# Both inputs of a two-part kernel transposed by DMA instead of by TensorE

## The chip, the core and the metric

The kernel runs on one core of a Trainium2 chip. The core has five engines that work side by side, each in the order of its own instruction queue: TensorE (PE; PEld are its weight loads), VectorE (DVE), ScalarE (ACT), GpSimd (POOL) and SyncE (SP), which here only issues DMAs. Matmul results land in PSUM, from where VectorE or ScalarE copies them to SBUF. The metric is the device time of one execution in microseconds (us).

## What is computed

Two independent parts share the launch, and their outputs are put side by side. Each has its own x of 2048 tokens by 448 features in bf16.

```python
# part A: a diagonal state space model, 448 complex states
Lam_bar = exp(dt * Lam);  B_bar = ((Lam_bar - 1) / Lam)[:, None] * Bmat
Bu = einsum("bld,pd->blp", x, B_bar)
h_t = Lam_bar * h_{t-1} + Bu_t                      # over 2048 tokens
y = 2 * einsum("blp,dp->bld", h, Cmat).real + x * Dskip
# part B: attention with 16 heads of 28, each token over 8 keys, 2 apart
q, k, v = split(x @ wqkv)
logits = q . k[s - 2 w] * scale, w = 0..7;  attn = softmax(logits)
out_b = (sum_w attn * v[s - 2 w]) @ wo
out = concat([y, out_b], -1)
```

## The kernel before, in words

TensorE contracts over the partitions (at most 128), so every product with x needs x with its features on the partitions. The kernel loads x with the tokens on the partitions (`load_x` of each part, L95 and L303; tiles `xb_sb` and `xa_sb`, which share the buffer "xin" one after the other) and turns it with TensorE: `transp` (L153 and L476) transposes eight blocks of 128 tokens by 112 features into a PSUM tile `pt_x` and one copy (`ev`, L73) takes it to `xT`. The 448 features stand as KT = 4 slabs of KP = 112.

**Part B** works in four chunks of 512 tokens. `proj_t` (L161, matmul L165) makes eight tiles of q and k per chunk, each 112 features by 512 tokens from four matmuls over the slabs; the weights `wn` come in three loads, k first (`load_w`). `qk` (L184) multiplies q with eight shifted views of k on VectorE (`pr`, L192), sums over each head's 28 features by matmuls with a matrix of ones (`lg`, L196), transposes the logits for their maximum (`pt_m`, L209; L210), subtracts it and takes exp. `proj_v` (L172) makes v for every sixteenth token per j; `halo` (L180) copies rows between partitions by DMA. `norm` (L220) normalises; `pv` (L236) multiplies and sums over the eight keys on VectorE (L249, L252), and `tail` (L256) transposes the result (`pt_o`), copies it (`oT`) and multiplies by wo (`wo_ps`, L269).

**Part A** puts token 16p + j on partition p. The 448 complex states are seven groups m of 64 states, real and imaginary parts on 128 partitions. `setup_b` (L445) multiplies B by a scale (`matg`) into `Bcat`, the weights of `local`. `local(b)` (L488, matmul L496) makes for each m a PSUM tile of 4 x 128 tokens (j = 4a + b) from four matmuls over the slabs, to which b = 1 and b = 3 add carried states (L499, L502); ScalarE copies it to `h[b]`. `setup_c` (L456) transposes C. `scan` (L511) runs the recurrence over 128 partition blocks on VectorE, `groups` (L556) and `correct(b)` (L571) bring its result back into the states, and `y` (L599) sums x times Dskip (a diagonal matrix `Dg`, L604) and the states times C (L607).

**What sets the order.** The body (L615) writes the order of the program; a scheduler keeps it as a priority and lets a later instruction go ahead on an engine when an earlier one is not ready, and then each engine's queue is fixed. `weave` (L662) runs a generator `main` and puts k steps of a `fill` between its steps: the projections and transposes of the next chunk go between the steps of `qk`, v between those of `qk(3)`, the transposes of part A's x between those of `local`. All large loads are issued on SyncE's queue in program order: B's x and weights, B and C of part A (`load_bc`), wo, later A's x. The small parameters go on ScalarE's queue (`load_params`). PSUM tiles come in three sets of buffers: "mm" (3), "pt" (2) and "lg" (3).

Of the kernel before, what the change touches and what calls it, by code (L numbers as in the profile page):

```python
# [31 lines left out]
PL = 64  # L32
MA = 4
# [54 lines left out]
class PartB:  # L88
# [6 lines left out]
    def load_x(self, n0, n1):  # L95
        if n0 == 0:
            self.x_sb = self.pool.tile([NCH, T, D], bf16, name="xb_sb", tag="xin")
        xv = self.B_x[0].rearrange("(n p) d -> p n d", p=NCH)
        self.nc.sync.dma_start(self.x_sb[:, n0:n1, :], xv[:, n0:n1, :])

    def load_w(self, which):
        if which == 1:
            self.wn = self.pool.tile([KP, KT, 3, D], bf16, name="wqkv_nat", tag="wn")
        v = self.B_wqkv.rearrange("(k p) (w c) -> p k w c", p=KP, w=3)
        self.nc.sync.dma_start(self.wn[:, :, which, :], v[:, :, which, :])
# [46 lines left out]

    def transp(self, n, eng):  # L153
        nc, cx = self.nc, self.cx
        pt = cx.ps([KP, KT, 2, NCH], bf16, "pt_x", "pt")
        for i in range(2):
            for k in range(KT):
                nc.tensor.transpose(pt[:, k, i, :], self.x_sb[:, n + i, k * KP:(k + 1) * KP], cx.ident[:])
        cx.ev(eng, self.xT[:, :, n * NCH:(n + 2) * NCH], pt[:].rearrange("p k i c -> p k (i c)"))
# [115 lines left out]
class PartA:  # L275
# [7 lines left out]
    def load_params(self):  # L283
        nc, pool = self.nc, self.pool
        self.prow = pool.tile([3 * NM, 2, PL], bf16, name="prow")
        self.drow = pool.tile([KT, KP], bf16, name="drow")
# [3 lines left out]
        nc.scalar.dma_start(self.drow[:], self.A_Dskip.rearrange("(k p) -> k p", p=KP))  # L290

    def load_bc(self):
        nc, pool = self.nc, self.pool
        self.bX = pool.tile([NCH, NM, D], bf16, name="bX")
        nc.sync.dma_start(self.bX[0:PL], self.A_Bre.rearrange("(m p) d -> p m d", p=PL))
        nc.sync.dma_start(self.bX[PL:NCH], self.A_Bim.rearrange("(m p) d -> p m d", p=PL))
        self.cn = pool.tile([KP, KT, NM, 2, PL], bf16, name="cn", tag="cn")
        for ri, src in enumerate((self.A_Cre, self.A_Cim)):
            v = src.rearrange("(a p) (m q) -> p a m q", p=KP, q=PL)
            for a in range(KT):  # L300
                nc.sync.dma_start(self.cn[:, a, :, ri, :], v[:, a])
# [16 lines left out]
    def params(self):  # L318
# [13 lines left out]
        ptd = self.cx.ps([KP, KT], bf16, "pt_d", "lg")  # L332
        nc.tensor.transpose(ptd[:], self.drow[:], ident[0:KT, 0:KT])
        dsk = sm("dsk", (KP, KT))
# [63 lines left out]
    def params_g(self):  # L398
        nc, G, ident = self.nc, self.nc.vector, self.cx.ident
        lre, lim, rden, Scat, dsk = self.lre, self.lim, self.rden, self.Scat, self.dsk  # L400
        la_re, la_im = self.pw_re[:, 0, :], self.pw_im[:, 0, :]

        def sm(name):
            return self.pool.tile([NCH, NM], f32, name=name)

        lm1, g_re, g_im, t1 = (sm(n) for n in ("lm1", "g_re", "g_im", "t1"))
        G.tensor_scalar(lm1[:], la_re, -1.0, None, op0=ALU.add)
        G.tensor_tensor(g_re[:], lm1[:], lre, op=ALU.mult)
        G.tensor_tensor(t1[:], la_im, lim, op=ALU.mult)
# [35 lines left out]
    def setup_b(self, engs):  # L445
        nc, cx, pool = self.nc, self.cx, self.pool
        self.Bcat = pool.tile([KP, KT, NM, NCH], bf16, name="Bcat")
        for i in range(NM):
            pt = cx.ps([KP, KT, NCH], f32, "pt_b", "pt")
            for k in range(KT):  # L450
                nc.tensor.matmul(pt[:, k, :], lhsT=self.bX[:, i, k * KP:(k + 1) * KP], rhs=self.mats["g"][:, i, :],
                                 start=(k == 0), stop=(k == KT - 1), skip_group_check=True)
            cx.ev(engs[i % len(engs)], self.Bcat[:, :, i, :], pt[:])
            yield
# [14 lines left out]
    def alloc(self):  # L469
        pool = self.pool  # L470
        xa = pool.tile([KP, 4, KT, 4, NCH], bf16, name="xaT", tag="xT")
        self.xT = {i: xa[:, i] for i in range(4)}
        u01 = pool.tile([NCH, 2, NM, 4 * NCH], bf16, name="u01", tag="q")
        self.h = [u01[:, 0], u01[:, 1], None, None]

    def transp(self, b, eng):  # L476
        nc, cx = self.nc, self.cx
        t_ = self.xT[b]
        for a in range(0, 4, 2):
            pt = cx.ps([KP, KT, 2, NCH], bf16, "pt_x", "pt")  # L480
            for i in range(2):
                for k in range(KT):
                    nc.tensor.transpose(pt[:, k, i, :], self.x_sb[:, 4 * (a + i) + b, k * KP:(k + 1) * KP],
                                        cx.ident[:])
            cx.ev(eng, t_[:, :, a:a + 2, :], pt[:])
            yield

    def local(self, b):  # L488
        nc, cx = self.nc, self.cx
        if b == 2:  # L490
            u23 = self.pool.tile([NCH, 2, NM, 4 * NCH], bf16, name="u23", tag="xin")
            self.h[2], self.h[3] = u23[:, 0], u23[:, 1]
        for m in range(NM):
            ps = cx.ps([NCH, 4 * NCH], f32, "u_ps", "mm")
            for k in range(KT):
                nc.tensor.matmul(ps[:], lhsT=self.Bcat[:, k, m, :], rhs=self.xT[b][:, k].rearrange("p a c -> p (a c)"),  # L496
                                 start=(k == 0), stop=(b % 2 == 0 and k == KT - 1))
# [13 lines left out]
    def scan(self):  # L511
# [6 lines left out]
        pc = [pool.tile(tab, bf16, name=f"pc{i}") for i in range(2)]  # L518
        psn = [pool.tile(tab, bf16, name=f"psn{i}") for i in range(2)]
# [79 lines left out]
    def y(self, a, b):  # L599
# [3 lines left out]
        for k in range(KT):  # L603
            nc.tensor.matmul(ps[:, k * KP:(k + 1) * KP], lhsT=self.xT[b][:, k, a, :], rhs=self.Dg[:, k, :],  # L604
# [10 lines left out]
def body(ctx: ExitStack, tc: tile.TileContext, A_x, A_Lre, A_Lim, A_Bre, A_Bim, A_Cre, A_Cim, A_logdt, A_Dskip,  # L615
# [25 lines left out]

    def transp(c):
        for n in range(0, 4, 2):
            b.transp(4 * c + n, "AV"[(n // 2) % 2] if c == 0 else "A")
            yield
# [48 lines left out]
    for b_ in (1, 0, 2):  # L694
        for _ in a.correct(b_, "A"):
# [39 lines left out]
```

## Time and profile before

| | |
|---|---|
| runs, median of 2 | 178.68 us (177.88 to 179.47) |
| the profiled execution | 177.29 us, its span 175.3 us |
| granted TensorE clock | 1.00 |
| busy: TensorE, VectorE, ScalarE, GpSimd | 159.6, 132.6, 108.9, 5.6 us |
| read from HBM, written | 6.89 MB, 3.67 MB |

The span runs from the first to the last instruction of the profiled execution. A row of the time line gives the start, the duration, the engine, the line of the kernel, the operation, the tiles written and read with partitions x elements, the count, and in brackets how long the engine had been idle before and what released it. In a row of the stretches stand the length, then the busy time (and the instructions) of PE, PEld, DVE, ACT and POOL, the granted clock, the mean busy share of the DMA engines and what they moved in GB/s. Matmuls are pipelined and their ends are modelled, so what a group of them costs is better read from the start of the next.

### The profile page before, as it was taken

Reading aid. Unit: us, or ns where it says so; the run is one execution under the profiler, and the core shown is the slowest. Engines: PE = TensorE matmul, PEld = TensorE weight load, DVE = VectorE, ACT = ScalarE, POOL = GpSimd, SP = SyncE. Lnnn points to the kernel's source line nnn. Section 1 sums busy time; section 2 is a strip of 40 time slices with the busy share of each in tenths; the row PEclk is TensorE's granted clock in tenths of the full one; section 3 lists DMA queues with packets and bytes.
Section 4 is the critical chain, followed back from the end, with each engine's and each line's share of the span. In section 5 each row is a group of like instructions: output and inputs, shape, how many; then the busy total and the mean of one; then the engine's idle time right before and its main releaser. Section 6 shows DMA issues by size and latency. Waiting matters only on the chain.

```text
span 175.3 us, 2965 instructions
## 1 busy us (share of the span) xinstructions
PE 159.6 (91%) x1171; PEld 90.8 (52%) x1175; DVE 132.6 (76%) x189; ACT 108.9 (62%) x183; POOL 5.6 (3%) x37
## 2 busy tenths in 40 slices
PE   7589798799799999999999999969999999999981
PEld 4355333445444766676565444746755455554550
DVE  1299998999996894039999999999999999900000
ACT  2279444775744876788899654356238739738382
POOL 8400000000000000000000000000000000000000
PEclk9999999999999999999999999999999999999999
DMA  5999851000370004170000000002111230140113
GB/s 155 291 297 179 90 119 30 0 4 0 87 332 0 6 0 109 50 200 8 0 4 0 0 0 0 4 0 77 33 52 52 79 108 26 52 132 30 52 54 105
DMA packets 16589, 12.36 MB, mean 70 GB/s; under 512 B 7219, under 2 KB 16065, under 8 KB 16575
## 3 DMA queue, kind: packets, MB, share of 16 engines
q1 hardware_dynamic: 16504, 12.16, 26.2%
q8 instruction: 9, 0.15, 0.4%
q14 instruction: 5, 0.04, 0.1%
q10 hardware_dynamic: 71, 0.01, 0.0%
HBM read 6.89 MB, written 3.67 MB: 60 GB/s over the span
## 4 chain that ended last, share of the span: by engine, by line
PE 51%; DVE 32%; ACT 10%; DMA 3%; issue 1%; ACTq 1%
PE y_ps L607 11%; PE qk_ps L165 11%; DVE pvb L252 9%; DVE pvt L249 8%; PE v_ps L177 7%; PE wo_ps L269 5%; PE lg L196 5%; DVE pr L192 4%; DMA drow<-in_A_Dskip_dram 3%; PE co L577 2%; ACT u L588 2%; DVE pvb L249 2%; PE y_ps L604 2%; ACT oT L264 2%; PE gt L566 1%
## 5 line engine op out<-in xcount | busy, mean ns | idle before, releaser
L192 DVE TENSOR_TENSOR pr<-qT,kT 112x2048 bf16<-112x2048 bf16 x32 | 37.0, 1219 | 0.5 <-ACT qT L77 0.5
L165 PE MATMUL qk_ps<-xbT,wqkv_nat 112*112 112x512 bf16 x128 | 32.3, 386 | 1.4 <-ACT xbT L77 1.1
L252 DVE TENSOR_TENSOR pvb<-pvb,pvt 128x1792 bf16<-128x1792 bf16 x28 | 30.3, 1083 | 0.0
L249 DVE TENSOR_TENSOR pvt<-attn,vd 128x1792 bf16<-128x1792 bf16 x28 | 30.0, 1083 | 0.0
L496 PE MATMUL u_ps<-xaT,Bcat 112*128 112x512 bf16 x112 | 27.4, 379 | 0.1
L503 ACT CAST u<-u_ps 128x512 bf16<-128x512 f32 x28 | 16.5, 590 | 9.2 <-PE u_ps L502 5.0
L165 PEld LDWEIGHTS <-wqkv_nat 112*112 112x112 bf16 x128 | 14.9, 129 | 14.1 <-issue 6.9
L607 PE MATMUL y_ps<-C,u 128*128 128x448 bf16 x84 | 18.0, 352 | 0.0
L610 ACT CAST ya<-y_ps 128x448 bf16<-128x448 f32 x16 | 8.5, 533 | 15.1 <-PE y_ps L607 14.2
L496 PEld LDWEIGHTS <-Bcat 112*128 112x128 bf16 x112 | 10.5, 97 | 10.8 <-issue 0.2
L269 PE MATMUL wo_ps<-wo_p,oT 112*128 112x448 bf16 x64 | 14.3, 353 | 1.0 <-ACT oT L264 0.9
L196 PE MATMUL lg<-pr,onesW 112*32 112x512 bf16 x128 | 12.8, 387 | 1.1 <-DVE pr L192 1.1
L177 PE MATMUL v_ps<-wqkv_nat,xbT 112*128 112x448 bf16 x64 | 13.7, 357 | 0.0
L77 ACT CAST kT<-qk_ps 112x512 bf16<-112x512 f32 x14 | 8.2, 584 | 8.1 <-PE qk_ps L165 8.1
L77 ACT CAST qT<-qk_ps 112x512 bf16<-112x512 f32 x14 | 8.2, 584 | 6.7 <-PE qk_ps L165 6.7
L271 ACT CAST yb<-wo_ps 128x448 bf16<-128x448 f32 x16 | 8.6, 539 | 5.8 <-PE wo_ps L269 5.6
L77 ACT CAST vd<-v_ps 128x448 bf16<-128x448 f32 x16 | 8.5, 533 | 4.5 <-PE v_ps L177 4.3
L177 PEld LDWEIGHTS <-xbT 112*128 112x128 bf16 x64 | 8.8, 146 | 4.0 <-issue 1.3
L210 DVE TENSOR_REDUCE mx<-pt_m 128x64 bf16<-128x512 bf16 x4 | 2.7, 687 | 10.5 <-PE pt_m L209 10.5
L588 ACT CAST u<-co 128x512 bf16<-128x512 f32 x21 | 10.6, 629 | 0.0
L607 PEld LDWEIGHTS <-u 128*128 128x128 bf16 x84 | 7.6, 97 | 5.5
L264 ACT COPY oT<-pt_o 112x1024 bf16<-112x1024 bf16 x8 | 8.1, 1047 | 2.5 <-PE pt_o L262 2.5
(175 smaller groups left out, 218.5 us busy)
## 6 DMA issues: line engine op xcount, KB each, us to landing
xb_sb<-in_B_x_dram SPq DMA_DIRECT2D x4, 448.0 KB, 7.0
xa_sb<-in_A_x_dram SPq DMA_DIRECT2D x2, 896.0 KB, 6.4
out_dram<-yb SPq DMA_DIRECT2D x8, 224.0 KB, 2.1
out_dram<-ya SPq DMA_DIRECT2D x16, 112.0 KB, 1.7
wqkv_nat<-in_B_wqkv_dram SPq DMA_DIRECT2D x3, 392.0 KB, 6.4
vd<-vd SPq DMA_DIRECT2D x1, 784.0 KB, 5.3
vd<-vd SPq DMA_DIRECT2D x1, 588.0 KB, 4.3
bX<-in_A_B_re_dram SPq DMA_DIRECT2D x1, 392.0 KB
```

What stands on the lines that cost most here:

```text
L77: nc.scalar.copy(out, in_)
L165: nc.tensor.matmul(ps[:], lhsT=self.wn[:, k, which, g * KP:(g + 1) * KP], rhs=self.xT[:, k, c * CH:(c + 1) * CH], start=(k == 0), stop=(k ...
L177: nc.tensor.matmul(ps[:], lhsT=xv[:, k, j, :], rhs=self.wn[:, k, 2, :], start=(k == 0), stop=(k == KT - 1))
L192: V.tensor_tensor(pr[:], self.qT[:, :, c * CH:(c + 1) * CH], self.kT[:, :, k0:k0 + CH], op=ALU.mult)
L196: nc.tensor.matmul(lg[NW * g:NW * (g + 1), :], lhsT=self.onesW[:, NW - 4 - 4 * w:2 * NW - 4 - 4 * w], rhs=pr[:, g, :], start=(w == 0), sto ...
L249: V.tensor_tensor(t_[:, 0:n], self.at[:, w, j0:j1, :].unsqueeze(2).to_broadcast([NCH, n, DH, H]), self.vd[:, off:off + n], op=ALU.mult)
L252: V.tensor_tensor(acc[:, 0:n], acc[:, 0:n], t_[:, 0:n], op=ALU.add)
L269: nc.tensor.matmul(ps[:], lhsT=oT[:, kt, i, :], rhs=self.wo_p[:, kt, :], start=(kt == 0), stop=(kt == KT - 1))
L496: nc.tensor.matmul(ps[:], lhsT=self.Bcat[:, k, m, :], rhs=self.xT[b][:, k].rearrange("p a c -> p (a c)"), start=(k == 0), stop=(b % 2 == 0 ...
L503: nc.scalar.copy(self.h[b][:, m, :], ps[:])
L588: nc.scalar.copy(h_, ps[:])
L607: nc.tensor.matmul(ps[:], lhsT=self.state(m, a, b), rhs=self.C[:, m, :], start=False, stop=(m == NM - 1), skip_group_check=True)
```

## The change

Nothing is transposed on TensorE for x any more. A DMA that transposes reads the source as rows and writes groups of 128 columns, each column on a partition.

- **Part B's x** comes in four pairs of transposing loads, one pair per chunk of 512 tokens: columns 0 to 383 as three slabs of 128, and columns 320 to 447 as a fourth, whose first 64 columns are there already. The rows of `wn` that meet them are set to zero, so the contraction has four slabs of 128. Each third of wqkv comes as two loads (384 rows and 64 rows).
- **Part A's x** comes in one transposing load: partition p's 16 tokens of 448 features are 7168 columns, that is 56 slabs of 128, seven for each pair of tokens. A token of even j uses the slabs 0 to 3 of its pair, of odd j 3 to 6; the middle slab is half the one's and half the other's. `Bcat` gets a version for each (`v`), with zeros at the half that isn't its own (two clears on GpSimd), so `setup_b` makes 14 groups instead of 7, their copies taking turns between ScalarE and VectorE. The load of `bX` gets 64 columns more, `Dskip` comes in four loads, and `Dg` has seven blocks instead of four.
- `a.load_x()` moves to the end of the first loads; its tile no longer shares a buffer with part B's x. `u23` takes the buffer of part B's `xT`, and the scan's four tables the buffer of `Bcat`.
- `setup_c` moves from `local(1)` into `local(0)`, and `correct(2)` adds on VectorE (`"V"`): without the identity matmul, and with a VectorE addition instead of the copy by ScalarE.

```diff
-    def load_x(self, n0, n1):
-        if n0 == 0:
-            self.x_sb = self.pool.tile([NCH, T, D], bf16, name="xb_sb", tag="xin")
-        xv = self.B_x[0].rearrange("(n p) d -> p n d", p=NCH)
-        self.nc.sync.dma_start(self.x_sb[:, n0:n1, :], xv[:, n0:n1, :])
+    def load_x(self, c):
+        if c == 0:
+            self.xT = self.pool.tile([NCH, KT, S], bf16, name="xbT", tag="xT")
+        sl = slice(c * CH, (c + 1) * CH)
+        x_ = self.B_x[0][sl, :]
+        self.nc.sync.dma_start_transpose(out=self.xT[:, 0:3, sl], in_=x_[:, 0:3 * NCH])
+        self.nc.sync.dma_start_transpose(out=self.xT[:, 3, sl], in_=x_[:, D - NCH:D])
...
+            self.wn = self.pool.tile([NCH, KT, 3, D], bf16, name="wqkv_nat", tag="wn")
+            self.nc.gpsimd.memset(self.wn[0:PL, 3], 0.0)
+        v = self.B_wqkv.rearrange("r (w c) -> r w c", w=3)[:, which, :]
+        self.nc.sync.dma_start(self.wn[:, 0:3, which, :], v[0:3 * NCH].rearrange("(k p) c -> p k c", p=NCH))
+        self.nc.sync.dma_start(self.wn[PL:NCH, 3, which, :], v[3 * NCH:D])
...
-        self.x_sb = self.pool.tile([NCH, T, D], bf16, name="xa_sb", tag="xin")
-        xv = self.A_x[0].rearrange("(p j) d -> p j d", j=T)
-        for g in range(2):
-            self.nc.sync.dma_start(self.x_sb[:, 8 * g:8 * g + 8, :], xv[:, 8 * g:8 * g + 8, :])
+        self.xs = self.pool.tile([NCH, NSL * T // 2, NCH], bf16, name="xaT", tag="xin")
+        self.nc.sync.dma_start_transpose(out=self.xs[:], in_=self.A_x[0].rearrange("(p j) d -> p (j d)", j=T))
+
+    def slab(self, j, k):
+        return self.xs[:, NSL * (j // 2) + 3 * (j % 2) + k, :]
...
-        self.Bcat = pool.tile([KP, KT, NM, NCH], bf16, name="Bcat")
+        self.Bcat = pool.tile([NCH, 2, KT, NM, NCH], bf16, name="Bcat")
         for i in range(NM):
...
+            for v in range(2):
+                pt = cx.ps([NCH, KT, NCH], f32, "pt_b", "pt")
+                for k in range(KT):
+                    d0 = SLAB[3 * v + k]
+                    nc.tensor.matmul(pt[:, k, :], lhsT=self.bX[:, i, d0:d0 + NCH], rhs=self.mats["g"][:, i, :],
+                                     start=(k == 0), stop=(k == KT - 1), skip_group_check=True)
+                cx.ev(engs[(2 * i + v) % len(engs)], self.Bcat[:, v, :, i, :], pt[:])
+                yield
+        nc.gpsimd.memset(self.Bcat[PL:NCH, 0, 3], 0.0)
+        nc.gpsimd.memset(self.Bcat[0:PL, 1, 0], 0.0)
...
+                s0 = NSL * (b // 2) + 3 * (b % 2) + k
+                nc.tensor.matmul(ps4[:], lhsT=self.Bcat[:, b % 2, k, m, :], rhs=self.xs[:, s0::2 * NSL, :],
                                  start=(k == 0), stop=(b % 2 == 0 and k == KT - 1))
...
-    b.load_x(0, 4)
+    b.load_x(0)
     b.load_w(1)
     b.load_w(0)
-    b.load_x(4, 8)
-    b.load_x(8, 12)
-    b.load_x(12, 16)
+    b.load_x(1)
+    b.load_x(2)
+    b.load_x(3)
     b.load_w(2)
     a.load_bc()
     b.load_wo()
+    a.load_x()
...
-    for _ in chain(transp(0), proj(0), transp(1)):
+    for _ in proj(0):
         pass
-    weave(b.qk(0), chain(proj(1), transp(2)), 2)
-    weave(b.qk(1), chain(proj(2), transp(3)), 2)
+    weave(b.qk(0), proj(1), 2)
+    weave(b.qk(1), proj(2), 2)
     a.params_g()
-    weave(b.qk(2), chain(proj(3), a.setup_b("A")), 2)
-    a.load_x()
+    weave(b.qk(2), chain(proj(3), a.setup_b("AV")), 2)
     weave(b.qk(3), vproj(), 4)
...
-    for _ in a.transp(0, "A"):
-        pass
-    weave(a.local(0), chain(a.transp(1, "A"), a.transp(2, "A")))
-    weave(a.local(1), chain(a.transp(3, "A"), a.setup_c("A")))
-    for b_ in (2, 3):
+    weave(a.local(0), a.setup_c("A"))
+    for b_ in (1, 2, 3):
...
-        for _ in a.correct(b_, "A"):
+        for _ in a.correct(b_, "V" if b_ == 2 else "A"):
```

More of the change, by code (lines that the diff above doesn't have):

```diff
@@ L32 @@
 PL = 64
+NSL = 7
+SLAB = [0, NCH, 2 * NCH, 3 * NCH, PL, PL + NCH, PL + 2 * NCH]
 MA = 4
@@ L151, in zero_halo @@
                                self.cx.wz[0:1, 0:D].unsqueeze(1).to_broadcast([1, HALO, D]))
[L153 to L159, printed above, removed]
     def proj_t(self, c, g, which, eng):
@@ L285, in load_params @@
         self.prow = pool.tile([3 * NM, 2, PL], bf16, name="prow")
-        self.drow = pool.tile([KT, KP], bf16, name="drow")
+        self.drow = pool.tile([NSL, NCH], bf16, name="drow")
         for i, src in enumerate((self.A_logdt, self.A_Lre, self.A_Lim)):
@@ L331, in params @@
         lre, lim = ll[:, 0], ll[:, 1]
-        ptd = self.cx.ps([KP, KT], bf16, "pt_d", "lg")
-        nc.tensor.transpose(ptd[:], self.drow[:], ident[0:KT, 0:KT])
-        dsk = sm("dsk", (KP, KT))
+        ptd = self.cx.ps([NCH, NSL], bf16, "pt_d", "lg")
+        nc.tensor.transpose(ptd[:], self.drow[:], ident[0:NSL, 0:NSL])
+        dsk = sm("dsk", (NCH, NSL))
         V.tensor_copy(dsk[:], ptd[:])
@@ L416, in params_g @@
         self.mat("g", self.rot_rows("Sg", g_re, g_im)[:], G)
-        self.Dg = self.pool.tile([KP, KT, KP], bf16, name="Dg")
-        for k in range(KT):
-            nc.scalar.activation(self.Dg[:, k, :], ident[0:KP, 0:KP], ACT.Copy, scale=dsk[:, k:k + 1])
+        self.Dg = self.pool.tile([NCH, NSL, NCH], bf16, name="Dg")
+        for k in range(NSL):
+            nc.scalar.activation(self.Dg[:, k, :], ident[:], ACT.Copy, scale=dsk[:, k:k + 1])
     def params_m(self):
@@ L469, in alloc @@
     def alloc(self):
[L470 to L486, printed above, removed]
+        u01 = self.pool.tile([NCH, 2, NM, 4 * NCH], bf16, name="u01", tag="q")
@@ L488, in local @@
+        u23 = self.pool.tile([NCH, 2, NM, 4 * NCH], bf16, name="u23", tag="xT")
+        self.h = [u01[:, 0], u01[:, 1], u23[:, 0], u23[:, 1]]
     def local(self, b):
         nc, cx = self.nc, self.cx
-        if b == 2:
-            u23 = self.pool.tile([NCH, 2, NM, 4 * NCH], bf16, name="u23", tag="xin")
-            self.h[2], self.h[3] = u23[:, 0], u23[:, 1]
         for m in range(NM):
-            ps = cx.ps([NCH, 4 * NCH], f32, "u_ps", "mm")
+            ps4 = cx.ps([NCH, 4, NCH], f32, "u_ps", "mm")
+            ps = ps4[:].rearrange("p a c -> p (a c)")
@@ L495, in local @@
             for k in range(KT):
-                nc.tensor.matmul(ps[:], lhsT=self.Bcat[:, k, m, :], rhs=self.xT[b][:, k].rearrange("p a c -> p (a c)"),
+                s0 = NSL * (b // 2) + 3 * (b % 2) + k
+                nc.tensor.matmul(ps4[:], lhsT=self.Bcat[:, b % 2, k, m, :], rhs=self.xs[:, s0::2 * NSL, :],
                                  start=(k == 0), stop=(b % 2 == 0 and k == KT - 1))
             if b % 2:
-                nc.tensor.matmul(ps[:], lhsT=self.mats[1][:, m, :], rhs=self.h[b - 1][:, m, :], start=False,
+                nc.tensor.matmul(ps, lhsT=self.mats[1][:, m, :], rhs=self.h[b - 1][:, m, :], start=False,
@@ L500, in local @@
                                  stop=(b == 1))
             if b == 3:
-                nc.tensor.matmul(ps[:], lhsT=self.mats[2][:, m, :], rhs=self.h[1][:, m, :], start=False, stop=True)
-            nc.scalar.copy(self.h[b][:, m, :], ps[:])
+                nc.tensor.matmul(ps, lhsT=self.mats[2][:, m, :], rhs=self.h[1][:, m, :], start=False, stop=True)
+            nc.scalar.copy(self.h[b][:, m, :], ps)
             yield
@@ L517, in scan @@
         tab = [NCH, NM, NCH]
-        pc = [pool.tile(tab, bf16, name=f"pc{i}") for i in range(2)]
-        psn = [pool.tile(tab, bf16, name=f"psn{i}") for i in range(2)]
+        rt = pool.tile([NCH, 4, NM, NCH], bf16, name="rt", tag="Bcat")
+        pc, psn = (rt[:, 0], rt[:, 1]), (rt[:, 2], rt[:, 3])
         g = pool.tile(tab, f32, name="gsc")
@@ L603, in y @@
         for k in range(KT):
-            nc.tensor.matmul(ps[:, k * KP:(k + 1) * KP], lhsT=self.xT[b][:, k, a, :], rhs=self.Dg[:, k, :],
+            i = 3 * (b % 2) + k
+            c0, c1 = (0, NCH) if i != 3 else (PL, NCH) if b % 2 else (0, PL)
+            d0 = i * NCH + c0 - (D if b % 2 else 0)
+            nc.tensor.matmul(ps[:, d0:d0 + c1 - c0], lhsT=self.slab(j, k), rhs=self.Dg[:, i, c0:c1],
                              start=(k == 0), stop=False, skip_group_check=True)
@@ L640, in body @@
     a.params()
[L642 to L645, printed above, removed]
     def proj(c):
```

24 lines of the change are left out of this document (10 added, 14 removed).

## The prediction

> **What bounds the kernel now.** I read the page first, then the stretches, then single rows in order of time. On the page, the busy shares, the slices and the chain that ended last:
>
> ```profile
> span 175.3 us, 2965 instructions
> PE 159.6 (91%) x1171; PEld 90.8 (52%) x1175; DVE 132.6 (76%) x189; ACT 108.9 (62%) x183; POOL 5.6 (3%) x37
> PE   7589798799799999999999999969999999999981
> DVE  1299998999996894039999999999999999900000
> PE 51%; DVE 32%; ACT 10%; DMA 3%; issue 1%; ACTq 1%
> ```
>
> TensorE is full nearly from start to end; VectorE is full in two long stretches. The stretches (columns: length, PE, PEld, DVE, ACT, POOL, clock, DMA share, GB/s) say how they share the path:
>
> ```profile
> 0.00:10.00 10.00, 6.28 (x63) 3.97 (x64) 2.88 (x19) 2.68 (x4) 5.61 (x37) 1.00 0.85 238
> 10.00:18.50 8.50, 7.62 (x42) 4.61 (x41) 8.05 (x21) 8.10 (x16) 0.00 (x0) 1.00 1.21 210
> 18.50:30.00 11.50, 10.94 (x65) 4.32 (x64) 11.50 (x16) 4.67 (x9) 0.00 (x0) 1.00 0.48 81
> 57.50:75.50 18.00, 17.92 (x136) 11.82 (x135) 9.97 (x10) 13.13 (x25) 0.00 (x0) 1.00 0.14 40
> 83.00:114.80 31.80, 30.91 (x210) 16.79 (x212) 31.80 (x33) 22.02 (x35) 0.00 (x0) 1.00 0.00 1
> 122.00:153.00 31.00, 30.65 (x236) 18.26 (x235) 30.69 (x35) 18.80 (x36) 0.00 (x0) 1.00 0.19 61
> ```
>
> Until 18.5 part B's first chunk waits for data and for ScalarE. From 57.5 to 75.5 TensorE alone is full. From 83 on both are, but VectorE's attention work ends at 153, and what follows is TensorE's. So time taken from TensorE shortens the span where VectorE doesn't hold it.
>
> **The change, part by part.** *Transposes and their copies.* All 128 TensorE transposes and 16 PSUM copies go. What one group of eight costs TensorE is its distance to the next work, not its modelled 0.61:
>
> ```profile
> 83.66 0.61 PE L483 MATMUL pt_x<-ident,xa_sb 128*112 128x128 bf16 x8
> 84.11 3.62 PE L496 MATMUL u_ps<-xaT,Bcat 112*128 112x512 bf16 x16
> PE pt_x L158 <- DVE mx L210: 0.9, 2, 0.7
> PE pt_x L483 <- DVE mx L210: 0.3, 1, 0.3
> ```
>
> It is 0.45 us. Part A has eight groups, 8 x 0.45 = 3.6, plus 0.3 that they waited for a PSUM buffer: **3.9**. Three of them lie in the wait for the last chunk's softmax; local(0) can use that time instead, so I count them in full. Part B's chunks 2 and 3 have four groups: 1.8, plus 0.9 of the same wait: **2.7**. The copies go from ScalarE, all but one, but outside the start it is not full (13.13 of 18, 22.02 of 31.8), so I count nothing there.
>
> *The start.* In order of time:
>
> ```profile
> 9.44 0.51 PEld L158 LDWEIGHTS <-xb_sb 128*112 128x112 bf16 x8 [1.81 <-DMA xb_sb<-in_B_x_dram]
> 9.94 6.21 PE L165 MATMUL qk_ps<-xbT,wqkv_nat 112*112 112x512 bf16 x28
> 16.48 1.02 PE L165 MATMUL qk_ps<-xbT,wqkv_nat 112*112 112x512 bf16 x4 [0.34 <-ACT qT L77]
> 18.56 9.17 DVE L192 TENSOR_TENSOR pr<-qT,kT 112x2048 bf16<-112x2048 bf16 x8
> 19.06 0.81 PE L165 MATMUL qk_ps<-xbT,wqkv_nat 112*112 112x512 bf16 x3 [1.10 <-ACT xbT L77]
> wqkv_nat<-in_B_wqkv_dram SPq DMA_DIRECT2D x3, 392.0 KB, 6.4
> 1.30 1.06 SPq L105 DMA_DIRECT2D wqkv_nat<-in_B_wqkv_dram  x2
> DMA to landing us min/median/max: 4.0/7.0/7.9
> ```
>
> The last row is xb_sb's. Now the first projection starts at 9.94, held by transposes of the second x block. Afterwards it needs chunk 0 and wk, which lands at 1.30 + 6.4 = 7.7 today. Chunk 0 grows from 458 to 524 thousand bytes, since 64 columns come twice. No row shows a transposing load; I bound it by plain loads. At the 238 GB/s of the first stretch it takes 2.2 instead of 1.9 us (+0.3). Its source runs are 256 bytes; the shortest in the trace are C's, of 128 bytes:
>
> ```profile
> 9.04 8.56 SPq L301 DMA_DIRECT2D cn<-in_A_C_re_dram x4
> ```
>
> That is 401 thousand bytes in 3,136 runs: 47 GB/s, or 2.73 ns a run. By runs chunk 0 (2,048) takes 5.6 us (+3.7). But in that stretch all loads together moved 210 GB/s, so C's issues mostly stood behind earlier traffic; I take 210 GB/s, 2.5 us (+0.6). Chunk 0 and wk also need two issues more, ahead of wk's last part, at 0.53 each (+0 to 1.0, taken 0.5). Start of projection 7.7 + 1.1 = 8.8, between 8.0 and 12.4: **1.1** gained (1.9 to -2.5). After the chunk's last matmul at 17.5 TensorE now does one transpose group and waits for its copy until 19.06; it will go straight on, **1.5**.
>
> [...]
>
> *Bcat twice.* Seven more groups of four matmuls, and seven PSUM copies on VectorE:
>
> ```profile
> 57.63 0.39 PE L451 MATMUL pt_b<-matg,bX 128*112 128x128 bf16 x4
> 57.86 0.93 PE L177 MATMUL v_ps<-wqkv_nat,xbT 112*128 112x448 bf16 x4
> 75.78 0.69 DVE L210 TENSOR_REDUCE mx<-pt_m 128x64 bf16<-128x512 bf16 x1 [7.97 <-PE pt_m L209]
> ```
>
> A group shifts TensorE by 0.23: 7 x 0.23, **-1.6**, in a full stretch. The copies, 7 x 0.68 (as L531's row below, 128x512 from PSUM), go into VectorE's 8 us of idle time before 75.78; without that cover they would cost 4.8. GpSimd's new clears cost nothing: wn's padding lies among its start work, well before chunk 0 lands, and Bcat's at a time when it has nothing else (0.00 in all later stretches).
>
> *K of 128 instead of 112* leaves the count and the 512 columns of each matmul as they are: nothing. Dskip's load lands at 2.10 + 4.39 = 6.5 (its issue, and its row in the chain):
>
> ```profile
> 2.10 0.32 ACTq L290 DMA_DIRECT2D drow<-in_A_Dskip_dram  x1
> 2.10 4.39 DMA drow<-in_A_Dskip_dram
> ```
>
> Three issues more at 0.32 make that 7.5, still ahead of 8.8; the larger Dg is no input of anything before y. *setup_c* moves from local(1) to local(0), the same work in the same full stretch; u23, rt and C reuse buffers whose readers come earlier on TensorE anyway.
>
> *correct(2)* loses seven identity matmuls and its seven additions go to VectorE:
>
> ```profile
> 157.26 0.81 PE L577 MATMUL co<-u,ident 128*128 128x512 bf16 x2
> 157.94 3.53 ACT L588 CAST u<-co 128x512 bf16<-128x512 f32 x7
> 160.54 0.36 PE L604 MATMUL y_ps<-Dg,xaT 112*128 112x112 bf16 x4
> 114.78 0.68 DVE L531 TENSOR_TENSOR pc<-g3A,cosE 128x512 bf16<-128x512 f32 x1
> 166.63 1.06 PE L262 MATMUL pt_o<-ident,pvb 128*112 128x128 bf16 x16
> ```
>
> The stage is 3.3 us now. The matmuls shrink to 1.7, but three PSUM buffers tie them to the additions, about 0.6 each pipelined and 4.2 in all; y's accumulators come from the same buffers. Bounds: 1.6 gained, or, if each addition queues behind one attention multiply, 7 x (0.6 + 1.08) - 3.3 = 8.5 lost. Those multiplies end at 153 and move earlier, and ScalarE is relieved: I take **0**.
>
> *A's x* no longer waits for part B to release its buffer; SyncE's queue, which today stands at that load, has the halo copies behind it:
>
> ```profile
> 5.18 0.98 SPq L105 DMA_DIRECT2D wqkv_nat<-in_B_wqkv_dram  x1
> 26.50 0.96 SPq L150 DMA_DIRECT2D vd<-wz  x1
> 78.84 1.24 PE L496 MATMUL u_ps<-xaT,Bcat 112*128 112x512 bf16 x5
> ```
>
> The loads between wv and the halo take SyncE 26.50 - 5.18 = 21.3 us. With 3.93 MB of transposing loads at 210 GB/s (18.7) and 4.2 of start (0.8, 1.1 of issues, 2.1 fixed, that is 4.0 less 1.9 of data) A's x is there by about 44, needed at 78.84 less the 3.7 gained by then, 75.1. Nothing.
>
> **Sum:** 1.1 + 1.5 + 2.7 - 1.6 + 3.9 + 0 = 7.6. The profiled execution took 177.29 us, its span plus 2.0, and becomes 169.7. The runs' median, 178.68, is 1.4 higher; on that level I forecast **171.1**, with a range of its own of 167 to 174.5.
>
> **The rivals.** *VectorE holds part B* (chance 0.19). For it: 11.50 of 11.5 busy while pr runs. Its only wait for TensorE in the first three chunks is this:
>
> ```profile
> 57.84 0.69 DVE L210 TENSOR_REDUCE mx<-pt_m 128x64 bf16<-128x512 bf16 x1 [2.51 <-PE pt_m L209]
> ```
>
> Then part B gains just 1.1 and those 2.5, less the 1.6 of Bcat; with A's 3.9 the gain is 5.9: 172.8, and 176.4 if the first load also comes out at its slow bound (-2.5 instead of 1.1). Against it: v_ps can fill TensorE while it waits for pr.
>
> *correct(2) waits behind the attention multiplies* (0.05): 171.1 + 8.5 = 179.6. Against it: VectorE has 13 us between its last multiply and the matching transposes at 166.63.
>
> *A's x comes late* (0.13): slower. Place: local(0)'s first matmul, with all of part A behind it. A's x lands at 4.2 + 21.3 + 3.93 MB / rate; it decides below 79 GB/s, and eats the whole gain of 7.6 below 69. At C's 47 GB/s it lands at 109, 30.3 after 78.84. Meanwhile TensorE can only bring forward part B's output matmuls:
>
> ```profile
> L269 PE MATMUL wo_ps<-wo_p,oT 112*128 112x448 bf16 x64 | 14.3, 353 | 1.0 <-ACT oT L264 0.9
> ```
>
> 177.3 + 30.3 - 14.3 - 3.9 = 189.4, or 191 on the median's level. For it: the short runs. Against it: the 210 GB/s beside C's loads. [...] I leave it 0.03 of the 0.13.
>
> *More than the sum* (0.05): the freed time of ScalarE were worth something outside the start, or the identity matmuls' 1.6, with the fast bound of the first load: 171.1 - 1.6 - 0.8 = 168.7, and below.
>
> **How the numbers follow.** The forecast has 0.58, the others as given. A measurement of this kernel tells about 2% from no change, that is 175.1 and 182.3. Faster: 0.58 + 0.05 + 0.15 of the first rival = 0.78. Same: 0.04 of it, 0.05 for correct(2), 0.01 of late x (just below the deciding rate): 0.10. Slower: 0.12. The range, 166 to 179.6, reaches to the correct(2) case and leaves out late x and a little below.
>
> **What would show it.** Right: no pt_x rows; first qk_ps near 8.8 and first pr near 17.4; 28 more pt_b rows and still no wait of pr for a copy; the last chunk's pt_m near 72; first u_ps before the tp matmuls, with A's x long landed; u_ps still 0.22 apart; TensorE full to the end. Wrong: a wait of u_ps for the DMA of A's x; SyncE's transposing issues of several us each with wk behind them; u_ps slower with its strided slabs; TensorE idle before pr or in correct(2).

## The result, and the profile after

The changed kernel takes **166.97 us** (median of 2 runs, 166.88 to 167.07) against 178.68: ratio 0.9345, interval 0.9165 to 0.9525, so faster. The forecast was 171.1 within 166 to 179.6, with 167 to 174.5 as its own range. Profiled against profiled it is 177.29 to 166.88, a gain of 10.4 where the sum said 7.6; the remaining 1.3 of the medians' 11.7 is level: the two runs of after lie 0.2 apart, those of before 1.6.

The page of after (its span, the busy time of the engines, two rows of the slices, and the chain that ended last):

```profile
span 165.2 us, 2764 instructions
PE 154.3 (93%) x1066; PEld 83.6 (51%) x1068; DVE 140.1 (85%) x202; ACT 92.1 (56%) x164; POOL 8.5 (5%) x40
PE   6799899999999999999999999889999999987990
...
PE 44%; DVE 41%; ACT 6%; issue 3%; DMA 2%; SPq 2%; DVEq 0%
```

TensorE lost 5.3 us of work and VectorE gained 7.5. On the chain, VectorE's share went from 32% to 41% and TensorE's from 51% to 44%. The stretches of after (columns as before: length, PE, PEld, DVE, ACT, POOL, clock, DMA share, GB/s) show it stage by stage:

```profile
7.20:16.80 9.60, 9.35 (x43) 5.34 (x44) 7.04 (x26) 6.63 (x18) 0.59 (x3) 1.00 0.99 200
30.00:57.50 27.50, 27.50 (x183) 13.00 (x181) 24.96 (x38) 15.61 (x28) 0.00 (x0) 1.00 0.58 108
57.50:70.90 13.40, 13.28 (x117) 8.24 (x115) 11.91 (x15) 8.67 (x17) 1.68 (x2) 1.00 0.15 40
79.40:110.60 31.20, 29.64 (x186) 15.41 (x186) 31.20 (x41) 17.34 (x29) 0.00 (x0) 1.00 0.02 8
110.63:147.47 36.84, 36.27 (x280) 21.65 (x279) 36.84 (x42) 21.05 (x38) 0.00 (x0) 1.00 0.19 64
149.44:165.20 15.76, 11.63 (x81) 6.47 (x81) 4.18 (x7) 6.18 (x10) 0.00 (x0) 0.93 0.17 59
```

In the stage of the last chunk (the third row) VectorE is now busy 11.91 of 13.4; the prediction's row for that stage had 9.97 of 18. From 79.4 on it has no idle time until its last attention multiply.

**Where the 10.4 us came from.** Three instants split both spans: the first `pr`, the end of the last attention multiply, and the last matmul with wo. Before (timeline; a row is start and length):

```profile
150.97 2.21 DVE L252 TENSOR_TENSOR pvb<-pvb,pvt 128x1792 bf16<-128x1792 bf16 x2
168.38 3.20 PE L269 MATMUL wo_ps<-wo_p,oT 112*128 112x448 bf16 x16 [0.69 <-ACT oT L264]
```

After, the same timeline rows, and between them correct(2)'s first matmuls and its additions, and the first transposes that wait for VectorE's end:

```profile
147.23 2.21 DVE L249 TENSOR_TENSOR pvb<-pvb,pvt 128x1792 bf16<-128x1792 bf16 x2
147.47 0.59 PE L573 MATMUL co<-u,mat 128*128 128x512 bf16 x2
149.35 4.27 DVE L583 TENSOR_TENSOR u<-co,u 128x512 bf16<-128x512 f32 x7
149.49 0.32 PE L259 MATMUL pt_o<-ident,pvb 128*112 128x128 bf16 x2 [1.43 <-DVE pvb L249]
158.94 2.25 PE L266 MATMUL wo_ps<-wo_p,oT 112*128 112x448 bf16 x11
```

The multiplies end at 153.18 and 149.44, the last matmul at 171.58 and 161.19. So the start gave 18.56 - 16.77 = 1.79, VectorE's stretch 134.62 - 132.67 = 1.95, and what TensorE has left behind it 18.40 - 11.75 = **6.65**; together 10.39. Before, TensorE was 18 us behind when VectorE was done. After, it waits for VectorE (the 1.43 in the row): the bound has moved. The same three numbers sort all the experiments (us, from each one's profile):

| kernel | first `pr` | first `pr` to last multiply | multiply to last wo matmul | last wo matmul ends |
|---|---|---|---|---|
| before | 18.56 | 134.62 | 18.40 | 171.58 |
| after | 16.77 | 132.67 | 11.75 | 161.19 |
| only_b | 16.95 | 130.54 | 17.01 | 164.50 |
| only_a | 21.51 | 137.26 | 13.70 | 172.47 |
| pe_back | 17.62 | 133.58 | 15.23 | 166.43 |
| act_back | 21.96 | 131.38 | 11.76 | 165.10 |
| act_late | 20.05 | 131.39 | 11.83 | 163.27 |
| act_tied | 18.27 | 132.65 | 12.72 | 163.64 |
| one_bcat | 16.51 | 130.19 | 11.75 | 158.45 |
| bcat_scalar | 18.41 | 130.35 | 13.73 | 162.49 |
| c2_scalar | 16.60 | 132.68 | 12.33 | 161.61 |
| wk_late | 20.97 | 132.65 | 11.75 | 165.37 |
| params_first_dg | 15.45 | 132.63 | 11.76 | 159.84 |
| best_b | 15.49 | 130.36 | 13.35 | 159.20 |

In four of them (act_back, act_tied, bcat_scalar, wk_late) and in only_a the first projection ran at half pace in the profiled execution (0.43 to 0.48 us for each of its first `qk_ps`, 0.24 in after), which puts 1.4 to 2.5 us into the first column (the last section); their medians may mix both paces.

### The profile page after: what moved, and what is told of

Read it like the earlier page. It is cut to its first block, busy times and chain, and to the rows that moved or that the text cites. A ratio compares the mean times of both kernels' runs of the same rounds, so it can differ in the third digit from the quotient of the medians.

```text
span 165.2 us, 2764 instructions
## 1 busy us (share of the span) xinstructions
PE 154.3 (93%) x1066; PEld 83.6 (51%) x1068; DVE 140.1 (85%) x202; ACT 92.1 (56%) x164; POOL 8.5 (5%) x40
## 2 busy tenths in 40 slices
DMA packets 30821, 12.72 MB, mean 77 GB/s; under 512 B 23756, under 2 KB 30554, under 8 KB 30808
## 4 chain that ended last, share of the span: by engine, by line
PE 44%; DVE 41%; ACT 6%; issue 3%; DMA 2%; SPq 2%; DVEq 0%
PE qk_ps L162 16%; DVE pvt L246 16%; DVE pvb L249 16%; PE v_ps L174 8%; PE lg L193 7%; PE y_ps L603 3%; DVE pvb L246 2%; PE u_ps L489 2%; DMA wqkv_nat<-in_B_wqkv_dram 2%; PE wo_ps L266 2%; PE pt_b L457 2%; DVE gsc L533 1%; DVE Gt L561 1%; DVE u L583 1%; ACT C L79 1%
## 5 line engine op out<-in xcount | busy, mean ns | idle before, releaser
L162 PE MATMUL qk_ps<-xbT,wqkv_nat 128*112 128x512 bf16 x128 | 32.4, 386 | 1.3 <-DMA wqkv_nat<-in_B_wqkv_dram 0.9
L489 PE MATMUL u_ps<-xaT,Bcat 128*128 128x512 bf16 x112 | 27.7, 379 | 0.1
L162 PEld LDWEIGHTS <-wqkv_nat 128*112 128x112 bf16 x128 | 14.9, 129 | 13.7 <-issue 4.8
L489 PEld LDWEIGHTS <-Bcat 128*128 128x128 bf16 x112 | 10.6, 98 | 11.5 <-issue 0.2
L174 PE MATMUL v_ps<-wqkv_nat,xbT 128*128 128x448 bf16 x64 | 15.9, 363 | 0.0
L193 PE MATMUL lg<-pr,onesW 112*32 112x512 bf16 x128 | 13.9, 389 | 0.5 <-DVE cs L388 0.4
L266 PE MATMUL wo_ps<-wo_p,oT 112*128 112x448 bf16 x64 | 13.6, 353 | 0.4 <-ACT oT L261 0.2
L174 PEld LDWEIGHTS <-xbT 128*128 128x128 bf16 x64 | 8.1, 147 | 4.0 <-issue 2.5
L193 PEld LDWEIGHTS <-onesW 112*32 112x32 bf16 x128 | 3.7, 93 | 11.4 <-issue 10.7
L266 PEld LDWEIGHTS <-oT 112*128 112x128 bf16 x64 | 5.9, 98 | 6.7 <-ACT oT L261 2.0
```

The costliest lines, as they stand in the source:

```text
L162: nc.tensor.matmul(ps[:], lhsT=self.wn[:, k, which, g * KP:(g + 1) * KP], rhs=self.xT[:, k, c * CH:(c + 1) * CH], start=(k == 0), stop=(k ...
L174: nc.tensor.matmul(ps[:], lhsT=xv[:, k, j, :], rhs=self.wn[:, k, 2, :], start=(k == 0), stop=(k == KT - 1))
L193: nc.tensor.matmul(lg[NW * g:NW * (g + 1), :], lhsT=self.onesW[:, NW - 4 - 4 * w:2 * NW - 4 - 4 * w], rhs=pr[:, g, :], start=(w == 0), sto ...
L266: nc.tensor.matmul(ps[:], lhsT=oT[:, kt, i, :], rhs=self.wo_p[:, kt, :], start=(kt == 0), stop=(kt == KT - 1))
L489: nc.tensor.matmul(ps4[:], lhsT=self.Bcat[:, b % 2, k, m, :], rhs=self.xs[:, s0::2 * NSL, :], start=(k == 0), stop=(b % 2 == 0 and k == KT ...
```

## The experiments

Each ratio is against the runs of before made beside that experiment on the same chip; "after" is 166.97. After itself was not run again, and before's median moved by about 1 us from session to session (178.68 with the result, 177.66 beside the first four experiments), so a difference of medians across sessions carries that much of level.

**The two halves alone.** only_b is the kernel before with part B's loads and projections as changed; only_a has part A's changes alone. In short (of only_b):

```diff
-    for _ in chain(transp(0), proj(0), transp(1)):
+    for _ in proj(0):
...
-    weave(b.qk(0), chain(proj(1), transp(2)), 2)
+    weave(b.qk(0), proj(1), 2)
```

> Part B's x by transposing loads, part A as before (its x turned by TensorE, one Bcat, correct(2) on ScalarE). Theory 1 (TensorE's time and the waits around its transposes are the gain): in the changed kernel the last chunk's pt_m came 4.7 us earlier although Bcat's extra 1.6 lay ahead of it, so part B alone is worth 6.3: 172.4 against 178.7. Theory 3 (the gain of part B is its earlier first projection, 2.8 us): 176.

> Part A's change alone (with Bcat twice, setup_c moved, correct(2) on VectorE), part B's x turned by TensorE as before. Theory 1: from pt_m of the last chunk to the scan the changed kernel was 5.2 us shorter; less Bcat's 1.6 that is 3.6: 175.1. If both parts add up, 6.3 + 3.6 = 9.9 is the whole gain. Rival: VectorE's attention work sets the end, its start does not move without part B's change, and part A alone is worth under 1.5: above 177.

only_b: 171.5 us, ratio 0.9665 (0.9594 to 0.9736). only_a: 176.86, 0.9949 (0.9903 to 0.9994). Part B's half is worth 6.2 against the 177.66 of before beside it and 7.2 against 178.68; the theory's 6.3 lies between, and the rival's 176 is far off. only_a came out 1.8 above its theory, near the rival. In its profile, of an execution of 178.22, the first projection is slow:

```profile
10.39 9.72 PE L167 MATMUL qk_ps<-xbT,wqkv_nat 112*112 112x512 bf16 x32
```

Before does the same 32 matmuls in 6.21 + 1.02. The 2.5 us of difference are put to the half pace (a granted clock of 0.50 from 11 to 14 us), not to part A. From the first `pr` on, only_a takes 150.96 against before's 153.02: part A's half alone is worth 2.1 there and 0.8 by the medians side by side, nearer the rival's 1.5 than the theory's 3.6. On top of part B's half it is worth more. From only_b to after it takes the tail from 17.01 to 11.75 and pays 2.1 in the middle column, where the second Bcat stands; the last matmul comes 3.3 earlier (4.5 by the medians).

**The transposes back on TensorE alone.** pe_back keeps the changed kernel and adds the old number of transposes (128, of the identity) where they stood, with nothing reading them.

```diff
+    def back(n):
+        for _ in range(n):
+            pt = cx.ps([KP, KT, 2, NCH], bf16, "pt_x", "pt")
+            for i in range(2):
+                for k in range(KT):
+                    nc.tensor.transpose(pt[:, k, i, :], cx.ident[:, 0:KP], cx.ident[:])
+            yield
```

> The changed kernel plus 16 groups of eight TensorE transposes of a constant, at the places where the old ones stood, without copies out of PSUM. Theory 1: 16 x 0.45 = 7.2, of which the two groups ahead of the first projection are hidden: +6.3, 173.3 against 167.0. Theory 2 (the gain is ScalarE's freed time): +0 to 1.

172.37 us, ratio 0.9743 (0.9665 to 0.9822): 5.4 lost of the 6.3 expected. Its timeline rows:

```profile
148.99 2.21 DVE L249 TENSOR_TENSOR pvb<-pvb,pvt 128x1792 bf16<-128x1792 bf16 x2
...
164.18 2.25 PE L266 MATMUL wo_ps<-wo_p,oT 112*128 112x448 bf16 x11
```

VectorE ends 1.76 later than in after (0.85 before the first `pr`, 0.91 from there on), TensorE 5.24 later. So most of the transposes' cost is not seen where they stand; it is 3.5 us of other TensorE work pushed behind VectorE's end. The first two groups are not quite in their old place: they run at 9.2, among the first projection's matmuls, where the expectation had them hidden ahead of it.

**The copies back on ScalarE alone.** Three kernels write the old copies' size to a scratch tile. act_back has all 16, act_late leaves out the four of the start, and act_tied reads data of the stage in which each copy belongs.

```diff
+            nc.scalar.copy(scr[:], cx.wz[0:KP].unsqueeze(1).to_broadcast([KP, 2, 4 * NCH]))
...
+            src = b.qT[:, 2:4, c * CH:(c + 1) * CH] if c else b.e[0:KP, 2 * CH:].rearrange("p (a n) -> p a n", a=2)
+            nc.scalar.copy(scr[:], src)
```

> The changed kernel plus 16 ScalarE copies of 112x1024, about 1.0 us each, at the places where the old copies stood, and no transposes. Theory 1: nothing, at most +1 (in the start, where ScalarE was 8.0 of 8.5 us busy): 167 to 168. Theory 2: most of the gain goes, +6 or more: 173.

> The changed kernel plus only the 12 later ScalarE copies of act_back; the four around the first projection are left away. With all 16 the first pr came 5.2 us later and the later points stayed 3.4 to 4.7 behind. Theory S (only the start is short of ScalarE): nothing, 167.0 to 167.5. Rival (each copy takes its part): 12/16 of 3.1, that is 169.3.

> The changed kernel with twelve ScalarE copies of the size of the old ones (1,024 elements a row, written to a scratch tile nobody reads), each tied by its data to the stage in which the old one stood: two read the queries of chunk 1, two those of chunk 2, eight read the exponentials of the last chunk and stand among part A's first u copies. The start has none. If ScalarE's relief is worth something at the start only, as the prediction said, the median is 167.0 to 167.5 and the first pr stays near 16.8. If the relief in the middle is what made the gain larger than the sum, 168.5 or more, with TensorE waiting for u copies (PSUM buffers) near 70 to 85.

act_back: 170.03 us, 0.9586 (0.9515 to 0.9656), between its two theories; its tail is after's, so the loss lies ahead of VectorE's end. act_late: 169.12, 0.953 (0.9444 to 0.9615), as its rival said. But act_late was no test of its question. Its copies read zeros, so nothing held them, and the scheduler drew them to the front (one group of its trace; start of the first and last at the end):

```profile
L664 ACT COPY scr<-wz x12: 1027/1048/1087, 5.2 to 32.1; 112x1024 bf16<-112x1024 bf16 x12
```

They sat in the start (first `pr` 20.05), which it was meant to spare. act_back's 16 drifted in the same way, to 5.2 to 45.4. act_tied's stand where they should:

```profile
L665 ACT COPY scr<-e_all x8: 1079/1128/1155, 76.1 to 87.3; 112x1024 bf16<-112x1024 bf16 x8
L665 ACT COPY scr<-qT x4: 1045/1047/1058, 26.8 to 41.1; 112x1024 bf16<-112x1024 bf16 x4
```

act_tied: 167.77 us (167.6 to 169.85), 0.9458 (0.9391 to 0.9525), 0.8 over after, between the two expectations. Its middle column is after's, 132.65 against 132.67: part B's copies cost nothing. The tail is 12.72 against 11.75: eight copies among the u copies slow part A's first states, and TensorE takes that 1.0 behind VectorE's end. So the prediction's count of nothing outside the start was off by up to 1 us, at a place that it did not look at.

**Bcat once.** one_bcat leaves out the odd version of Bcat; odd tokens of part A use the even one, so part A's output is another. The seven copies that stay take turns, four on ScalarE and three on VectorE, so VectorE has four fewer.

```diff
-            for v in range(2):
+            for v in range(1):
```

> The changed kernel with Bcat made once: tokens of odd j use the even version, so part A's output is another. Theory 1 (TensorE's order sets the end): the seven groups' 1.6 us, or the 2.4 by which the last pt_m lay behind that of only_b: 164.6 to 165.4. Rival (VectorE's attention work sets the end now): its first multiply moves by the seven copies at most, under 1: 166 to 167.

164.38 us, 0.9243 (0.9188 to 0.9298): the second Bcat costs **2.6**, not 1.6. It doesn't tell TensorE's groups from the copies; the next experiment moves only the copies. Its timeline:

```profile
144.49 2.21 DVE L249 TENSOR_TENSOR pvb<-pvb,pvt 128x1792 bf16<-128x1792 bf16 x2
...
156.20 2.25 PE L266 MATMUL wo_ps<-wo_p,oT 112*128 112x448 bf16 x11
```

VectorE ends 2.74 earlier, and the tail is after's to a hundredth: in after the end hangs on VectorE.

**Bcat's copies on ScalarE.** bcat_scalar leaves nothing out.

```diff
-    weave(b.qk(2), chain(proj(3), a.setup_b("AV")), 2)
+    weave(b.qk(2), chain(proj(3), a.setup_b("A")), 2)
```

> The changed kernel with all fourteen copies of Bcat on ScalarE, none on VectorE; nothing left out. Theory that the second Bcat costs 2.6 rather than 1.6 because its VectorE copies delay the last chunk's multiplies: 1.0 faster, 166.0, with the last pt_m near 69.7. Theory that the whole cost is TensorE's (fourteen groups instead of seven): 167.0, last pt_m unmoved at 70.7. ScalarE then has 8.75 + 7 x 0.59 = 12.9 of 13.5 us in 57.5 to 71, so it may also become the bound there: then above 167.

166.74 us (165.98 to 168.21), 0.9381 (0.9315 to 0.9447). VectorE's stretch shortens by 2.3, as the theory of its copies wants, even more than the 1.0. But the end gains little, because the tail grows by 2.0: freed of VectorE, the end hangs on TensorE again. From the first `pr` on it is 144.08 against 144.42, that is 0.3. The gain is below what these runs separate.

**correct(2) as before.** c2_scalar gives the seven identity matmuls back to TensorE and the sums to ScalarE.

```diff
-        for _ in a.correct(b_, "V" if b_ == 2 else "A"):
+        for _ in a.correct(b_, "A"):
```

> The changed kernel with correct(2) as before: seven identity matmuls on TensorE and the sums copied by ScalarE. The prediction counted this part at 0 within -1.6 and +8.5. If 0 is right: 167.0 within 0.4. If the additions on VectorE were a gain by the identity matmuls' 1.6: 168.6. If they cost something because they wait behind the attention multiplies: faster than 166.6.

167.57 us (167.28 to 169.73), 0.9445 (0.9377 to 0.9513): 0.6 more than after, and 0.6 in the tail (12.33 against 11.75). The additions on VectorE look like a gain of about 0.6, between the forecast's 0 and its bound of 1.6. The wait behind the multiplies did come, but once and not seven times: in after two `co` matmuls stand at 147.47, the first addition starts at 149.35, when the last multiplies are done, and TensorE sits idle for the 1.43 shown above. In c2_scalar TensorE has no such wait. The interval is wider than the difference; the tail is the better witness.

**The load that the first projection waits for.** wk_late puts part B's second block of x ahead of the k weights.

```diff
     b.load_x(0)
+    b.load_x(1)
     b.load_w(1)
     b.load_w(0)
-    b.load_x(1)
```

> The changed kernel with the second chunk's transposing loads ahead of the weights on SyncE's queue, so that wk lands about 2.8 us later. Theory D (the first projection's start passes on in full): +2.8, 169.8. Theory S (the start is short of ScalarE and VectorE, whose parameter work runs meanwhile): the first pr moves by less than half of it, +1.4 at most: 167 to 168.4.

171.32 us, 0.9646 (0.9571 to 0.9722), 1.5 beyond the theory of a delay passed on. The first `qk_ps` starts 2.81 later than in after, at 9.99, as forecast:

```profile
9.99 2.38 PE L162 MATMUL qk_ps<-xbT,wqkv_nat 128*112 128x512 bf16 x5 [3.63 <-DMA wqkv_nat<-in_B_wqkv_dram]
```

But five matmuls take 2.38 us where after's nine take 2.15: half pace. With it the first `pr` is 4.20 late, and the end exactly as much, 4.18.

**The parameters first.** params_first_dg puts the transpose of part A's parameters ahead of the first projection on TensorE, and Dskip's transpose and `Dg` away from the start.

```diff
-    for _ in proj(0):
-        pass
+    with tc.issue_after(a.ptp.ins):
+        for _ in proj(0):
+            pass
...
+    a.params_d()
     a.scan()
```

> The changed kernel with the transpose of part A's parameters ahead of the first projection on TensorE (it stood nine matmuls behind it) and Dskip's transpose and the seven copies of Dg (2.8 us of ScalarE) taken out of the start to before the scan. Theory S: the parameter work begins about 2 us earlier and the first pr comes 2 to 3 us earlier: 164 to 165. Theory D: the first projection doesn't move: 167.

165.57 us, 0.9332 (0.9254 to 0.941), half a microsecond above its theory's 164 to 165. The first `qk_ps` stands at 7.11, as in after, the first `pr` 1.32 earlier, the end 1.35.

**Both together.** best_b has that and Bcat's copies on ScalarE.

> The parameter transpose ahead of the first projection and Dskip's transpose moved to part A's setup (as in the run params_first_dg), and all copies of Bcat on ScalarE. If both gains add: 166.97 - 1.4 - 1.0 = 164.6, first pr near 15.5, last pt_m near 68.4. If the copies of Bcat are no gain: 165.6.

**164.91 us**, 0.9281 (0.9223 to 0.9338), 2.1 under after of the 2.4 that adding gives; the best kernel here that leaves nothing out. Its middle column is bcat_scalar's (130.36 against 130.35), and its tail of 13.35, above 11.75, says that TensorE sets its end again.

## Why the prediction was right, and where it was not

**What bounds the kernel:** right for before ("what follows is TensorE's"). Not asked was when VectorE takes over. Removing TensorE time pays only down to the tail of 11.75 that stands behind VectorE's last multiply whatever TensorE does; after, one_bcat, wk_late, params_first_dg and act_back all end with it, and act_late within 0.1.

**The start, 1.1:** too small. Timeline of after, SyncE's queue first:

```profile
0.81 1.39 SPq L102 DMA_TRANSPOSE xbT<-in_B_x_dram  x1
2.26 1.51 SPq L103 DMA_TRANSPOSE xbT<-in_B_x_dram  x1
3.82 0.58 SPq L110 DMA_DIRECT2D wqkv_nat<-in_B_wqkv_dram  x1
...
7.18 2.15 PE L162 MATMUL qk_ps<-xbT,wqkv_nat 128*112 128x512 bf16 x9 [0.91 <-DMA wqkv_nat<-in_B_wqkv_dram]
9.26 0.18 PE L330 MATMUL pt_p<-ident,prow 21*128 21x21 bf16 x1
9.47 0.18 ACT L332 ACTIVATE dt_bf<-pt_p 128x7 bf16<-128x7 bf16 x1 [4.20 <-PE pt_d L337]
16.77 1.22 DVE L189 TENSOR_TENSOR pr<-qT,kT 112x2048 bf16<-112x2048 bf16 x1
17.99 1.08 DVE L391 TENSOR_TENSOR cosE<-shE 128x896 f32<-128x896 f32 x1
20.19 4.63 DVE L189 TENSOR_TENSOR pr<-qT,kT 112x2048 bf16<-112x2048 bf16 x4
```

The step that failed is the base of that term, "wk, which lands at 1.30 + 6.4 = 7.7 today", with "two issues more" at 0.53 each on top. The transposing issues hold SyncE 1.4 to 1.5 us each, and yet wk comes earlier: its issue is 2.5 us later, but the 6.4 became 3.3. Before, it shared the DMA engines with all the loads issued right behind it; now these are issued later (a reading of the order of the issues; no run isolates it). Two rows of after's issues (KB of one, median us from issue to landing) stand against the 6.4 of before:

```profile
wqkv_nat<-in_B_wqkv_dram SPq DMA_DIRECT2D x3, 336.0 KB, 3.3
...
xbT<-in_B_x_dram SPq DMA_TRANSPOSE x8, 3.9
```

So wk's first part lands at 3.82 + 3.3 = 7.1 and `qk_ps` starts at 7.18, 2.8 earlier and outside the bound of 8.0. The first `pr` gains 1.79 of it. The parameters' transpose now stands behind nine matmuls in TensorE's queue (9.26; ScalarE waited 4.20 for it), and params_first_dg, which also moves the copies of `Dg` away, gets 1.3 of the rest back.

**Straight on after chunk 0, 1.5:** not where it was put. VectorE's tables stand between the first `pr` and the second (20.19), and the chunk's `pt_m` comes just 0.68 earlier (31.07 to 30.39). The first rival, VectorE holding part B, was right for this chunk alone. The later chunks' `pt_m` gain 1.84, 2.51 and 4.68: TensorE brings v forward and is full, 27.50 of 27.5. For all of part B the sum had 3.7, the trace 4.68.

**Bcat twice, -1.6:** the TensorE part held where it can be read (64.48 to 64.70 and 66.20 to 66.43 from a `pt_b` group to the next work, 0.22 and 0.23). The cover failed: "VectorE's 8 us of idle time before 75.78". That time was a wait for TensorE, and it shrank when TensorE's transposes went. In order of time, in after:

```profile
65.74 1.22 DVE L189 TENSOR_TENSOR pr<-qT,kT 112x2048 bf16<-112x2048 bf16 x1
...
66.87 0.68 DVE L85 CAST Bcat<-pt_b 128x512 bf16<-128x512 f32 x1
...
67.47 1.22 DVE L189 TENSOR_TENSOR pr<-qT,kT 112x2048 bf16<-112x2048 bf16 x1
...
69.81 1.04 PE L489 MATMUL u_ps<-xaT,Bcat 128*128 128x512 bf16 x4
...
70.68 0.39 PE L206 MATMUL pt_m<-ident,lgb 128*128 128x128 bf16 x4
```

A copy stands between the last two `pr`, with no gap. It was named as the price without cover (4.8); one_bcat puts the whole second Bcat at 2.6, and bcat_scalar shortens VectorE's stretch by 2.3 by moving the copies alone.

**Part A, 3.9:** right in kind, small in size. From the last `pt_m` to the scan's first matmul it is 31.06 against 36.32: 5.3. The first `u_ps` starts at 69.81, ahead of `tp` at 74.34, with A's x long there, and 12 of them run before `tp`, as foreseen.

**A's x, 0:** right. After's queue holds one issue of 8.23 us; the stretch behind it shows the rate:

```profile
33.30 8.23 SPq L308 DMA_TRANSPOSE xaT<-in_A_x_dram  x1
```

```profile
36.00:44.00 8.00, 8.00 (x53) 3.43 (x52) 7.00 (x19) 4.08 (x8) 0.00 (x0) 1.00 1.34 207
```

The traffic ends by 44, as forecast, 25 us ahead of its first use, at 207 GB/s against the 210 that the prediction took. The late-x rival fell with it. The 0.03 of its 0.13 stood for blocks that go one after the other and far slower, a price that no run shows: A's x is 56 blocks of 128x128, 1.835 MB, and at 207 GB/s that is 8.9 us, an estimate of 158 ns each.

**correct(2), 0:** a gain of about 0.6 by c2_scalar, although one of the signs of being wrong, "TensorE idle before pr or in correct(2)", did show (the 1.43). Of the signs of being right, `u_ps` stands 0.22 apart and runs before `tp`, as said; the first `qk_ps` (7.18 for 8.8) and the last chunk's `pt_m` (70.7 for 72) came earlier, and TensorE is not full to the end: 11.63 of the last 15.76.

**The sum:** 7.6 against 10.4. The excess is 1.0 in part B with its start (4.68 for 3.7, in spite of Bcat's 2.6), 1.4 from there to the scan (5.3 for 3.9), and 0.4 behind it. Errors of both signs meet in it: Bcat cost 1.0 more than its term, and the rest together gave more than theirs. So 166.97 lies near the lower end of the stated range and just below the forecast's own. The case nearest to the result is the one called "more than the sum" (168.7, chance 0.05). It named ScalarE's time (0.8 by act_tied), the identity matmuls (0.6) and the first load's fast bound, which the load went beyond; these do not add up to the whole excess. The parts put back one by one (transposes 5.4, tied copies 0.8, correct(2) 0.6, less 2.6 for Bcat) make 4.2 and leave about 6 for the start and for what the parts do to each other. wk_late bears out 2.8 of that for the load, and copies drawn into the start cost act_late about 1.3 more than act_tied. The remaining 2 were not separated, and their cause stays open.

## What to carry to other kernels

Split the span at the end of the engine that will be the next bound: what shortens the work left behind that instant, and what moves the instant, are two accounts, and a saving pays in only one of them. An engine's idle time is cover only if its cause stays: when the wait is for the engine that the change relieves, the cover goes with it. Dummy copies without data to hold them drifted to the front here (act_late's to 5.2 to 32.1 us), so tie such an instruction to the stage that it is to load.

## What the runs showed of the hardware

**TensorE's pace at the start is not the same in all executions.** The first nine `qk_ps` took 2.15 us in after (0.24 each) and, in bcat_scalar, whose start has the same instructions:

```profile
7.06 3.91 PE L162 MATMUL qk_ps<-xbT,wqkv_nat 128*112 128x512 bf16 x9 [0.69 <-DMA wqkv_nat<-in_B_wqkv_dram]
```

That is 0.43 each. Where the records hold the change, the granted clock shows it; the stretch of act_back's first projection, and one of only_a's:

```profile
7.20:10.80 3.60, 3.60 (x9) 1.60 (x9) 0.00 (x0) 1.15 (x2) 0.59 (x3) 0.54 0.85 197
```

```profile
11.00:14.00 3.00, 3.00 (x9) 1.50 (x8) 1.59 (x3) 2.42 (x5) 0.00 (x0) 0.50 1.10 237
```

bcat_scalar's own stretch from 7.2 to 10.8 has 1.00, with its matmuls 0.43 apart all the same; so the matmuls' spacing is the surer sign. How long the half clock lasts is an estimate from the clocks of the stretches: about 3.4 us in act_back (0.54 from 7.2 to 10.8, 1.00 from 11 on) and in wk_late (0.84 from 7.2 to 10.8, 0.66 from 11 to 14, behind a wait of 3.63), and about 6.8 in only_a (0.74 from 7.2 to 10.8, 0.76 from 10 to 22). In wk_late the first `pr` is 4.20 late, 2.81 of it by the load and the remaining 1.4 put to the pace. No run shows what sets the pace, or why it changes from one execution to another. That a wait for data brings the half pace is not isolated: act_tied and bcat_scalar had it behind waits of 0.6 and 0.7 us, after did not behind 0.91, and only_a had it with transposes ahead of its first projection.

**A transposing load was dear to issue here and not slow to run.** In after it holds SyncE's queue 1.3 to 2.0 us for each of the two issues of a 512-token block, where the issues of wqkv take 0.49 to 0.59, and 8.23 for A's whole x. All loads together moved 200 GB/s from 7.2 to 16.8, with part B's x among them, and 207 from 36 to 44, while A's x came; the halo copies behind A's x were not needed sooner.
